# Logits with slots on partitions, slot sums in four column groups, and TensorE in the written order

## The chip, the cores and the metric

The kernel runs on one core of one Trainium2 chip. The metric is the device time in microseconds of one execution, inputs and output in the chip's memory. TensorE multiplies matrices (PE in the profile, its weight loads PEld), ScalarE (ACT), VectorE (DVE) and GpSimd (POOL) work on elements; here GpSimd issues all loads and SyncE (SP) the stores.

## The reference

Attention over a sliding window, and then a soft mixture of experts on its result:

```python
# q, k, v: 8 batches, 8 heads, 576 rows, 64 wide
scores = scale * q @ k.T, kept where 0 <= i - j < 64        # window
attn = softmax(scores) @ v
x = attn as (B*S, H*D) = (4608, 512)
logits = x @ phi                                            # phi: 512 x 32 (8 experts x 4 slots)
d = softmax of logits over the 4608 rows;  slot_input = d.T @ x      # 32 x 512
slot_out[e] = relu(slot_input[e] @ w1[e]) @ w2[e]           # w1: 512 x 1024, w2: 1024 x 512
c = softmax of logits over the 32 slots;   out = c @ slot_out        # 4608 x 512
```

## The kernel before

A **unit** is half a batch: four heads, 576 rows. There are 16, u = 2b + half. Each runs three **steps** j = 0, 1, 2 over windows of 64 queries (4, 4 and 1 windows). A step does `stage_t2` (transposes of v, line L177, copied to vw by L178), `stage_s` (a mask product, L188, and the scores, L195, summed in the one PSUM tile sc; then their exponential on ScalarE, L200, into pm), a third of the *next* unit's first transposes (`stage_t1`, L146: q in step 0, k in step 1, v in step 2; the copies out are L153 on ScalarE and for half of v L151 on VectorE), and `stage_av` of the step before (L223, then L229 to L241 on VectorE, into x_bp). So v of the next unit is transposed in step 2 and read by L177 at the next unit's start.

The mixture's work on a batch is cut into six pieces, one at the end of each step of the two units that follow: `stage_xt` three times (L258: transposes of x into xT), `stage_logit` (L269: 32 columns a matmul, rows on partitions; L273 exponential, written four times side by side into ex), `stage_slot` (L288: sums over the rows of ex times x and of ex times ones, 32 columns a matmul; L294 adds them to acc), `stage_et` (L301: ex transposed into ET). The last batch does them after the loop. An even batch has 4 chunks of 128 rows, an odd one 5. Then come the experts (L367, L374, L386 from the weights w1s and w2s; the last expert's w2 is w2l) and the output (L402 from ET, scaled by L406 and L408, stored by L411).

PSUM tiles tagged "tr" rotate over four buffers; sc and av have one each. A scheduler orders the instructions of each engine, but for those named in `manual_schedule`, which stay in the order in which the code issues them: GpSimd alone, before. Its queue holds the loads: `issue_loads(u)` issues q, k and v of unit u+3 and one half of an expert's weight, the rest of the weights all at unit 13.

Of the kernel before, what the change touches and what calls it, by code (L numbers as in the profile page):

```python
# [16 lines left out]
def kernel(  # L17
# [10 lines left out]
    nc = tc.nc  # L28

    B, H, S, Dh = q.shape  # L30
    D, NSLOT = moe_phi.shape
    E, _, F = moe_w1.shape
# [73 lines left out]
    ones = const.tile([128, 128], FP16, name="ones")  # L106
    nc.vector.memset(ones, 1.0)
# [19 lines left out]
    acc = const.tile([128, 5, NSLOT], FP32, name="acc")  # L127
# [118 lines left out]
    def moe_chunks(b):  # L246
        c = [4 * (b % 2) + i for i in range(4)]
        return c + [8] if b % 2 else c

    def stage_xt(b, part):  # L250
        xb = xbp[b // 2]
        ch = moe_chunks(b)[2 * part:2 * part + 2]
        if not ch:
            return
        tr = ps.tile([128, 8, 128], FP16, name="tr", tag="tr", bufs=4)
        for n, c in enumerate(ch):
            for kk in range(NHD):
                nc.tensor.transpose(tr[:, 4 * n + kk, :], xb[:, c, 128 * kk:128 * kk + 128], ident[:, :])  # L258
        xT = pxt.tile([128, 8, 128], FP16, name="xT", tag="xT")
        nc.vector.tensor_copy(out=xT[:, 0:4 * len(ch), :], in_=tr[:, 0:4 * len(ch), :])  # L260
        moe[b, part] = xT

    def stage_logit(b):
        ch = moe_chunks(b)
        lt = ps.tile([128, 5, NSLOT], FP32, name="lt", tag="tr", bufs=4)
        for n, c in enumerate(ch):
            xT = moe[b, n // 2]
            for kk in range(NHD):
                nc.tensor.matmul(lt[:, n, :], xT[:, 4 * (n % 2) + kk, :], phi_sb[:, kk, :],  # L269
                                 start=(kk == 0), stop=(kk == NHD - 1))  # L270
        nch = len(ch)
        ex = psm.tile([128, 5, 4, NSLOT], FP16, name="ex", tag="ex", bufs=2)
        nc.scalar.activation(ex[:, 0:nch, :, :],  # L273
                             lt[:, 0:nch, :].unsqueeze(2).broadcast_to([128, nch, 4, NSLOT]), AF.Exp)
        rs = psm.tile([128, 5], FP32, name="rs", tag="rs")
        nc.vector.reduce_sum(rs[:, 0:nch], ex[:, 0:nch, 0, :], axis=AXX)
        nc.vector.reciprocal(crcp[:, b, 0:nch], rs[:, 0:nch])
        moe["ex", b] = ex

    def stage_slot(b):  # L280
        ch = moe_chunks(b)
        xb = xbp[b // 2]
        ex = moe["ex", b]
        pa = ps.tile([128, 5, NSLOT], FP32, name="pa", tag="tr", bufs=4)
        for n, c in enumerate(ch):
            for dc in range(NHD + 1):
                lhs = xb[:, c, 128 * dc:128 * dc + 128] if dc < NHD else ones[:, :]
                nc.tensor.matmul(pa[:, dc, :], lhs, ex[:, n, 0, :],  # L288
                                 start=(n == 0 and dc == 0), stop=(n == len(ch) - 1 and dc == NHD),
                                 skip_group_check=True)  # L290
        if b == 0:
            nc.vector.tensor_copy(out=acc[:, :, :], in_=pa[:, :, :])
        else:
            nc.vector.tensor_tensor(out=acc[:, :, :], in0=pa[:, :, :], in1=acc[:, :, :], op=ALU.add)  # L294

    def stage_et(b):
        ex = moe["ex", b]
        nch = len(moe_chunks(b))
        te = ps.tile([128, 8, 128], FP16, name="te", tag="tr", bufs=4)
        for n in range(nch):  # L300
            nc.tensor.transpose(te[:, n, :], ex[:, n].rearrange("p r s -> p (r s)"), ident[:, :])  # L301
        nc.vector.tensor_copy(out=ET[:, 4 * b:4 * b + 4, :], in_=te[:, 0:4, :])
        if nch > 4:
            nc.vector.tensor_copy(out=ET[:, 4 * B + b // 2, :], in_=te[:, 4, :])


    nu = len(units)
# [13 lines left out]
    for u in range(nu):  # L321
        issue_loads(u)
        if u == nu - 3:
            while w_order:
                load_w(*w_order.pop(0))
        for j in range(3):
            stage_t2(u, j)
            stage_s(u, j)
            if u + 1 < nu:
                stage_t1(u + 1, j)  # L330
            if pend is not None:
                stage_av(*pend)
                pu, pj = pend
                if pj == 2 and units[pu][1] == 1:
                    b = units[pu][0]
                    todo += [lambda b=b: stage_xt(b, 0), lambda b=b: stage_xt(b, 1), lambda b=b: stage_xt(b, 2),
                             lambda b=b: stage_logit(b), lambda b=b: stage_slot(b), lambda b=b: stage_et(b)]
# [8 lines left out]
    stage_xt(b, 1)  # L346
    stage_xt(b, 2)
    stage_logit(b)
    stage_slot(b)
    stage_et(b)  # L350
# [4 lines left out]
    dinv = const.tile([128, NSLOT], FP32, name="dinv")  # L355
    nc.vector.reciprocal(dinv, acc[:, NHD, :])
    nc.vector.tensor_tensor(out=slot_inT[:, :, :], in0=acc[:, 0:NHD, :],
                            in1=dinv[:, :].unsqueeze(1).broadcast_to([128, NHD, NSLOT]), op=ALU.mult)
# [90 lines left out]
```

## Time and profile before

| | |
|---|---|
| three runs, median (lowest to highest) | 201.0 us (198.66 to 201.95) |
| the profiled execution: its time, its span | 200.05 us, 198.2 us |
| busy: TensorE, VectorE, ScalarE | 142.4, 109.3, 109.6 us |
| mean granted TensorE clock | 0.924 |
| loads on GpSimd's queue | 30.97 MB |
| TensorE matmuls (each with a weight load) | 3148 |

The span is from the first to the last instruction; the execution's own time has 1.85 us around it. Views of the trace are in us from the span's start. In the order of time a row has its start, its duration, engine, line, operation, output<-inputs, shapes and count, and in brackets how long the engine stood idle before it and for what. A matmul's duration holds some 0.18 us of latency, so matmuls in a row overlap and their spacing is what they cost. "issue" is time in which an engine waited for nothing that the profile shows.

### The profile page before, as it was taken

The numbers are of one execution on the slowest core, as the hardware profiler recorded it, in microseconds if no ns is written. First come the engines' busy times: TensorE is split into PE (matmuls) and PEld (weight loads), VectorE is DVE, ScalarE is ACT, GpSimd is POOL, SyncE is SP. The second block draws the span as 40 slices with busy tenths as digits, with TensorE's granted clock in tenths as the row PEclk, the third lists the DMA queues.
The fourth block names the chain that finished last, engine by engine and source line by source line (L and its number), as shares of the span: only waits on it lengthen the run. The fifth ranks groups of instructions, "written<-read, shape, count | busy, mean of one in ns | idle before, by whom it ended". The sixth has DMA issues, their size and how long they took to land.

```text
span 198.2 us, 7045 instructions
## 1 busy us (share of the span) xinstructions
PE 142.4 (72%) x3148; PEld 106.2 (54%) x3148; DVE 109.3 (55%) x268; ACT 109.6 (55%) x164; POOL 59.6 (30%) x89
## 2 busy tenths in 40 slices
PE   0599897778987879884999897698757873983000
PEld 0376776667766667764778676587644441220000
DVE  3026677558665757753787585578852112895000
ACT  2457976858575596765479486566311222894000
POOL 7945444423341424321442662222230000000000
PEclk9999999999999999998799999999985999698555
DMA  4999999999999999999699999999999992799995
GB/s 69 160 204 206 207 209 206 205 207 209 211 209 204 206 208 204 203 162 171 69 175 187 175 178 186 210 208 211 206 212 207 211 203 37 289 377 379 379 334 145
DMA packets 31309, 40.84 MB, mean 206 GB/s; under 512 B 2096, under 2 KB 22576, under 8 KB 31280
## 3 DMA queue, kind: packets, MB, share of 16 engines
q0 software_dynamic: 26384, 30.97, 93.5%
q1 hardware_dynamic: 4896, 9.44, 13.6%
q8 instruction: 24, 0.39, 0.7%
q14 instruction: 5, 0.04, 0.1%
HBM read 61.93 MB, written 9.44 MB: 360 GB/s over the span
## 4 chain that ended last, share of the span: by engine, by line
PE 43%; ACT 15%; DMA 13%; issue 11%; DVE 8%; POOL 1%; DVEq 0%; ACTq 0%; POOLq 0%
PE tr L146 11%; DMA w2l<-in_moe_w_dram 10%; PE tr L177 8%; ACT pm L200 7%; PE sc L188 6%; PE sc L195 5%; PE av L223 4%; DVE ob L408 4%; DMA kn<-in_k_dram 3%; ACT kT_125 L153 3%; PE tr L258 3%; ACT kT_116 L153 2%; PE cp L402 2%; PE lt L269 2%; ACT qT L153 2%
## 5 line engine op out<-in xcount | busy, mean ns | idle before, releaser
L200 ACT ACTIVATE pm<-sc 128x1024 f16<-128x1024 f32 (+1 forms) x48 | 39.5, 823 | 40.2 <-PE sc L195 37.4
L177 PE MATMUL tr<-ident,vT 128*128 128x128 f16 x288 | 24.9, 224 | 1.0 <-DVE rc L229 0.9
L153 ACT COPY qT<-tr 128x640 f16<-128x640 f16 (+1 forms) x32 | 21.9, 746 | 4.9 <-PE tr L146 4.9
L188 PE MATMUL sc<-rep,hide 64*128 64x512 f16 (+1 forms) x96 | 20.8, 339 | 2.5 <-ACT pm L200 1.3
L231 DVE TENSOR_TENSOR x_bp<-av,rc 128x512 f16<-128x512 f32 x32 | 22.0, 687 | 0.8
L177 PEld LDWEIGHTS <-vT 128*128 128x128 f16 x288 | 17.7, 100 | 4.8 <-issue 3.1
L223 PEld LDWEIGHTS <-pm 128*64 128x64 f16 x576 | 15.8, 112 | 6.9 <-issue 5.6
L151 DVE COPY vT<-tr 128x512 f16<-128x512 f16 x16 | 11.6, 724 | 12.9 <-PE tr L146 12.8
L61 POOL DMA_DIRECT2D vn<-in_v_dram x16 | 11.5, 716 | 23.0 <-PE av L223 14.6
L146 PE MATMUL tr<-ident,qn 128*64 128x128 f16 x288 | 12.3, 233 | 7.6 <-DMA qn<-in_q_dram 5.4
L61 POOL DMA_DIRECT2D qn<-in_q_dram x16 | 11.5, 717 | 20.7 <-PE av L223 14.2
L61 POOL DMA_DIRECT2D kn<-in_k_dram x16 | 11.5, 718 | 16.5 <-PE av L223 12.0
L178 DVE COPY vw_126<-tr 128x1024 f16<-128x1024 f16 (+1 forms) x24 | 13.3, 553 | 4.3 <-PE tr L177 4.2
L146 PE MATMUL tr<-ident,vn 128*64 128x128 f16 x288 | 13.8, 232 | 2.3 <-issue 0.7
L81 POOL DMA_DIRECT2D w1s<-in_moe_w_dram x16 | 11.5, 719 | 11.3 <-DMA w1s<-in_moe_w_dram 8.9
L178 DVE COPY vw_118<-tr 128x1024 f16<-128x1024 f16 (+1 forms) x24 | 13.2, 549 | 2.8 <-PE tr L177 2.8
L84 POOL DMA_DIRECT2D w2s<-in_moe_w_dram x14 | 10.6, 767 | 11.8 <-DMA w2s<-in_moe_w_dram 8.7
L146 PEld LDWEIGHTS <-qn 128*64 128x64 f16 x288 | 9.5, 117 | 8.5 <-DMA qn<-in_q_dram 5.4
L408 DVE TENSOR_SCALAR ob<-cp,crcp 128x512 f32<-128x512 f32 x18 | 12.6, 747 | 1.3 <-PE cp L402 1.0
L402 PE MATMUL cp<-slot_oa,ET 128*128 128x512 f16 x36 | 11.5, 425 | 2.4 <-ACT ob L406 1.3
L260 DVE COPY xT<-tr 128x1024 f16<-128x1024 f16 (+1 forms) x20 | 12.6, 628 | 1.0 <-PE tr L258 0.7
L146 PE MATMUL tr<-ident,kn 128*64 128x128 f16 x288 | 11.8, 228 | 1.8 <-DMA kn<-in_k_dram 1.8
(76 smaller groups left out, 258.2 us busy)
## 6 DMA issues: line engine op xcount, KB each, us to landing
out_dram<-ob SPq DMA_DIRECT2D x18, 512.0 KB, 5.5
w1s<-in_moe_w_dram POOLq DMA_DIRECT2D x16, 512.0 KB, 13.9
w2s<-in_moe_w_dram POOLq DMA_DIRECT2D x14, 512.0 KB, 13.5
qn<-in_q_dram POOLq DMA_DIRECT2D x16, 288.0 KB, 9.9
kn<-in_k_dram POOLq DMA_DIRECT2D x16, 288.0 KB, 9.6
vn<-in_v_dram POOLq DMA_DIRECT2D x16, 288.0 KB, 8.9
w2l<-in_moe_w_dram POOLq DMA_DIRECT2D x2, 512.0 KB, 19.7
phi_sb<-in_moe_phi_dram POOLq DMA_DIRECT2D x1, 32.0 KB, 7.8
```

The source lines that it names most:

```text
L61: nc.gpsimd.dma_start(out=t, in_=src[b, 4 * half:4 * half + 4].rearrange("(x h) (g t) d -> (h g) x (t d)", x=2, h=2, t=T))
L146: nc.tensor.transpose(tr[64 * x:64 * x + 64, j, :], src[:, x, 64 * (t0 + j):64 * (t0 + j) + 64], ident[:, :])
L153: nc.scalar.copy(out=o, in_=i)
L177: nc.tensor.transpose(tr[:, 2 * w + h, :], st["vT"][:, h, 64 * i:64 * i + 128], ident[:, :])
L178: nc.vector.tensor_copy(out=st["vw"][:, wins[0]:wins[0] + n, :, 0:64], in_=tr[:, 0:2 * n, :].rearrange("p (w h) (x d) -> p w (h x) d", h=2 ...
L188: nc.tensor.matmul(sc[:, x, 0:128 * n], hide[64 * x:64 * x + 64, :], rep[64 * x:64 * x + 64, 0:2 * n, :], start=True, stop=False, skip_gro ...
L200: nc.scalar.activation(pm[:, :, 0:2 * n, :], sc[:, :, 0:128 * n].rearrange("p x (w q) -> p x w q", q=64), AF.Exp, scale=scale)
L223: nc.tensor.matmul(av[r0:r0 + 64, kk, 65 * (w // 2):65 * (w // 2) + 65], pm[:, x, h * n + w, :], st["vw"][:, i, 2 * h + x, 0:65], start=Tr ...
L231: nc.vector.tensor_tensor(out=xb[:, c0:c0 + 2, 256 * half:256 * half + 256].rearrange("p c (k d) -> p k c d", d=64), in0=avv[:, :, :, 0:64 ...
L260: nc.vector.tensor_copy(out=xT[:, 0:4 * len(ch), :], in_=tr[:, 0:4 * len(ch), :])
L402: nc.tensor.matmul(cp[:, :], ET[:, 4 * blk + g, :], slot_oa[:, :], start=True, stop=True)
L408: nc.vector.tensor_scalar(out=ob[:, g, :], in0=cp[:, :], scalar1=cr, scalar2=None, op0=ALU.mult)
```

## The change

Seven things:

- **Logits** have slots on partitions: `stage_logit` multiplies phi4 (phi's 32 columns four times) with xT, 512 columns a matmul, four matmuls for a batch's first four chunks, and four of 128 columns for the fifth of an odd batch. The exponential goes straight into ET, and its sum over columns into esum. The layout of xT follows.
- **stage_ex** replaces stage_et, one piece earlier: matmuls of 32 columns turn ET's chunks back (te); ScalarE casts them to ex, VectorE sums them for crcp.
- **Slot sums** take ex (32 columns) as weights and x as the moving operand of 512 columns, chunk n in column group n % 4; acc is 128 x 512. The sums with ones are gone.
- **At the end** acc is scaled by 1/esum and the four groups are summed by four matmuls (si) with sel4 into slot_inT.
- **TensorE** joins GpSimd in `manual_schedule`.
- **Weights**: `issue_loads` issues two halves in place of one at u = 2, 5, 8 and 11.
- The pool of xT has one buffer of each tag in place of three.

```diff
-    pxt = ctx.enter_context(tc.tile_pool(name="pxt", bufs=3))
+    pxt = ctx.enter_context(tc.tile_pool(name="pxt", bufs=1))
...
+    sel4 = const.tile([128, NSLOT], FP16, name="sel4")
+        nc.vector.reduce_sum(sel4, ident.rearrange("p (g s) -> p s g", s=NSLOT), axis=AXX)
...
+    phi4 = const.tile([128, NHD, 4, NSLOT], FP16, name="phi4")
+    nc.vector.tensor_copy(out=phi4, in_=phi_sb.unsqueeze(2).broadcast_to([128, NHD, 4, NSLOT]))
...
-    psum1.enter_context(tc.manual_schedule(engines={mybir.EngineType.Pool}))
+    psum1.enter_context(tc.manual_schedule(engines={mybir.EngineType.Pool, mybir.EngineType.PE}))
...
     def stage_logit(b):
-        for n, c in enumerate(ch):
-            xT = moe[b, n // 2]
-            for kk in range(NHD):
-                nc.tensor.matmul(lt[:, n, :], xT[:, 4 * (n % 2) + kk, :], phi_sb[:, kk, :],
-                                 start=(kk == 0), stop=(kk == NHD - 1))
-        nc.scalar.activation(ex[:, 0:nch, :, :],
-                             lt[:, 0:nch, :].unsqueeze(2).broadcast_to([128, nch, 4, NSLOT]), AF.Exp)
+        for kk in range(NHD):
+            nc.tensor.matmul(lt[:, :], phi4[:, kk].rearrange("p r s -> p (r s)"), moe[b][:, kk],
+                             start=(kk == 0), stop=(kk == NHD - 1))
+        nc.scalar.activation(ET[:, 4 * b:4 * b + 4, :], lt[:, :].rearrange("p (c q) -> p c q", q=128),
+                             AF.Exp, accum_out=esum[:, b:b + 1])
+        if b % 2:
+            ...
+                nc.tensor.matmul(l8[:, :], phi4[:, kk].rearrange("p r s -> p (r s)"), moe[b, 8][:, kk],
+            ...
+            nc.scalar.activation(ET[:, 4 * B + b // 2, :], l8[:, :], AF.Exp,
+                                 accum_out=esum[:, B + b // 2:B + b // 2 + 1])
...
+    def stage_ex(b):
+        te = ps.tile([128, 5, NSLOT], FP32, name="te", tag="tr", bufs=4)
         for n, c in enumerate(ch):
+            nc.tensor.matmul(te[:, n, :], ET[:, c, :], ident[:, 0:NSLOT], start=True, stop=True)
+        nc.scalar.copy(out=ex[:, 0:nch, :], in_=te[:, 0:nch, :])
+        nc.vector.reduce_sum(rs[:, 0:nch], te[:, 0:nch, :], axis=AXX)
         nc.vector.reciprocal(crcp[:, b, 0:nch], rs[:, 0:nch])
...
     def stage_slot(b):
         for n, c in enumerate(ch):
-            for dc in range(NHD + 1):
-                lhs = xb[:, c, 128 * dc:128 * dc + 128] if dc < NHD else ones[:, :]
-                nc.tensor.matmul(pa[:, dc, :], lhs, ex[:, n, 0, :], ...
+            g = n % 4
+            nc.tensor.matmul(pa[32 * g:32 * g + 32, :], ex[:, n, :], xbp[b // 2][:, c, :],
+                             start=(n < 4), stop=(n + 4 >= len(ch)), skip_group_check=True)
...
-    def stage_et(b):
...
-            load_w(*w_order.pop(0))
+            for _ in range(2 if u % 3 == 2 else 1):
+                load_w(*w_order.pop(0))
...
+    nc.vector.reduce_sum(dinv[:, 0:1], esum[:, :], axis=AXX)
+    nc.vector.reciprocal(dinv[:, 1:2], dinv[:, 0:1])
+    nc.scalar.activation(pa_sb[:, 0:256], acc[:, 0:256], AF.Copy, scale=dinv[:, 1:2])
+    nc.vector.tensor_scalar(out=pa_sb[:, 256:512], in0=acc[:, 256:512], scalar1=dinv[:, 1:2], scalar2=None, op0=ALU.mult)
...
+    for dc in range(NHD):
+        nc.tensor.matmul(si[:, dc, :], pa_sb[:, 128 * dc:128 * dc + 128], sel4[:, :], start=True, stop=True)
+    nc.vector.tensor_copy(out=slot_inT, in_=si)
```

TensorE has 6298 instructions before and 5826 after. How they stand changes at three places of which the prediction speaks. Lines of attention are 5 higher in the changed kernel (L177 is L182, L188 L193, L195 L200, L200 L205, L223 L228).

TensorE at the boundary from unit 2 to unit 3, before: hide and rep make the mask product, kT and qT the scores, vT the transposes that read both copies of v. "..." stands for more of the same row.

```order
L223 MATMUL av<-vw_118,pm 64x65
L188 LDWEIGHTS hide
L188 MATMUL sc<-rep,hide 128x512
...
L195 LDWEIGHTS kT_125
L195 MATMUL sc<-qT,kT_125 128x64
...
L177 LDWEIGHTS vT
L177 MATMUL tr<-ident,vT 128x128
```

The same place in the change:

```order
L228 MATMUL av<-vw_118,pm 64x65
L182 LDWEIGHTS vT
L182 MATMUL tr<-ident,vT 128x128
...
L193 LDWEIGHTS hide
L193 MATMUL sc<-rep,hide 128x512
...
L200 LDWEIGHTS kT_125
L200 MATMUL sc<-qT,kT_125 128x64
```

Two mask products and three score products have moved from ahead of the eight transposes of vT to behind them. At boundaries into even units, before, one mask product stood ahead of the transposes and one behind.

ScalarE in an odd unit (u = 5, batch 1), before, from one first pm to the next:

```order
L200 ACTIVATE pm<-sc 128x1024
L153 COPY qT<-tr 128x128x5
L153 COPY qT<-tr 128x128x4
L273 ACTIVATE ex<-lt 128x640
L200 ACTIVATE pm<-sc 128x1024
L153 COPY kT_116<-tr 128x2x64x5
L153 COPY kT_116<-tr 128x2x64x4
L200 ACTIVATE pm<-sc 128x2x128
L153 COPY vT<-tr 128x2x64x5
```

and in the change:

```order
L205 ACTIVATE pm<-sc 128x1024
L158 COPY qT<-tr 128x128x5
L158 COPY qT<-tr 128x128x4
L280 ACTIVATE ET,esum<-lt 128x512
L287 ACTIVATE ET,esum<-l_1356 128x128
L205 ACTIVATE pm<-sc 128x1024
L158 COPY kT_116<-tr 128x2x64x5
L158 COPY kT_116<-tr 128x2x64x4
L301 CAST ex<-te 128x160
L205 ACTIVATE pm<-sc 128x2x128
L158 COPY vT<-tr 128x2x64x5
```

One exponential has become two, and a cast stands ahead of the third pm.

VectorE at the end, from the last batch's first xT copy to the experts' input, before:

```order
L260 COPY xT<-tr 128x1024
L237 RECIPROCAL rc<-av 64x4
L260 COPY xT<-tr 128x1024
L238 TENSOR_TENSOR x_bp<-av,rc 64x256
L260 COPY xT<-tr 128x512
L276 TENSOR_REDUCE rs<-ex 128x5
L277 RECIPROCAL crcp<-rs 128x5
L294 TENSOR_TENSOR acc<-pa,acc 128x160
L302 COPY ET<-te 128x512
L304 COPY ET<-te 128x128
L356 RECIPROCAL dinv<-acc 128x32
L357 TENSOR_TENSOR slot_inT<-acc,dinv 128x128
```

and in the change:

```order
L319 TENSOR_TENSOR acc<-pa,acc 128x512
L242 RECIPROCAL rc<-av 64x4
L268 COPY xT<-tr 128x4x256
L243 TENSOR_TENSOR x_bp<-av,rc 64x256
L268 COPY xT<-tr 128x4x256
L272 COPY xT_3698<-tr 128x512
...
L303 TENSOR_REDUCE rs<-te 128x5
L304 RECIPROCAL crcp<-rs 128x5
L319 TENSOR_TENSOR acc<-pa,acc 128x512
L373 TENSOR_SCALAR slot_oa<-acc,dinv 128x256
L381 CAST slot_inT<-si 128x128
```

The first acc of the change is that of batch 6, now ahead of the last batch's xT copies; the copies to ET are gone, and the scaling and the copy of si have come.

More of the change, by code (lines that the diff above doesn't have):

```diff
@@ L105 @@
             in_=ident[64 * h:64 * h + 64, 64 * h:64 * h + 64].unsqueeze(1).broadcast_to([64, 8, 64]))
-    ones = const.tile([128, 128], FP16, name="ones")
-    nc.vector.memset(ones, 1.0)
+    sel4 = const.tile([128, NSLOT], FP16, name="sel4")
+    with nc.allow_low_precision("sums of 0 and 1"):
+        nc.vector.reduce_sum(sel4, ident.rearrange("p (g s) -> p s g", s=NSLOT), axis=AXX)
     kTs, vTs, vws, hTs = [], [], [], []
@@ L254, in stage_xt @@
             return
+        nch = len(ch)
+        if part == 0:
+            moe[b] = pxt.tile([128, NHD, 4, 128], FP16, name="xT", tag="xT")
         tr = ps.tile([128, 8, 128], FP16, name="tr", tag="tr", bufs=4)
-        for n, c in enumerate(ch):
-            for kk in range(NHD):
-                nc.tensor.transpose(tr[:, 4 * n + kk, :], xb[:, c, 128 * kk:128 * kk + 128], ident[:, :])
-        xT = pxt.tile([128, 8, 128], FP16, name="xT", tag="xT")
-        nc.vector.tensor_copy(out=xT[:, 0:4 * len(ch), :], in_=tr[:, 0:4 * len(ch), :])
@@ new lines, in stage_xt, with stage_logit @@
+        if part < 2:
+            nc.vector.tensor_copy(out=moe[b][:, :, 2 * part:2 * part + 2, :],
+                                  in_=tr[:, :, :].rearrange("p (k n) q -> p k n q", n=2))
+        else:
+            moe[b, 8] = pxt.tile([128, NHD, 128], FP16, name="xT8", tag="xT8")
+            nc.vector.tensor_copy(out=moe[b, 8], in_=tr[:, 0:4, :])
+    def stage_logit(b):
+        lt = ps.tile([128, 512], FP32, name="lt", tag="tr", bufs=4)
+        for kk in range(NHD):
+            nc.tensor.matmul(lt[:, :], phi4[:, kk].rearrange("p r s -> p (r s)"), moe[b][:, kk],
[3 more added lines that the diff above has]
+        if b % 2:
+            l8 = ps.tile([128, 128], FP32, name="l8", tag="tr", bufs=4)
+            for kk in range(NHD):
+                nc.tensor.matmul(l8[:, :], phi4[:, kk].rearrange("p r s -> p (r s)"), moe[b, 8][:, kk],
+                                 start=(kk == 0), stop=(kk == NHD - 1))
+            nc.scalar.activation(ET[:, 4 * B + b // 2, :], l8[:, :], AF.Exp,
+                                 accum_out=esum[:, B + b // 2:B + b // 2 + 1])
@@ L280, in stage_slot @@
     def stage_slot(b):
+        ex = moe["ex", b]
+        pa = ps.tile([128, D], FP32, name="pa", tag="tr", bufs=4)
         ch = moe_chunks(b)
-        xb = xbp[b // 2]
-        ex = moe["ex", b]
-        pa = ps.tile([128, 5, NSLOT], FP32, name="pa", tag="tr", bufs=4)
         for n, c in enumerate(ch):
-            for dc in range(NHD + 1):
-                lhs = xb[:, c, 128 * dc:128 * dc + 128] if dc < NHD else ones[:, :]
-                nc.tensor.matmul(pa[:, dc, :], lhs, ex[:, n, 0, :],
-                                 start=(n == 0 and dc == 0), stop=(n == len(ch) - 1 and dc == NHD),
-                                 skip_group_check=True)
+            g = n % 4
+            nc.tensor.matmul(pa[32 * g:32 * g + 32, :], ex[:, n, :], xbp[b // 2][:, c, :],
+                             start=(n < 4), stop=(n + 4 >= len(ch)), skip_group_check=True)
         if b == 0:
-            nc.vector.tensor_copy(out=acc[:, :, :], in_=pa[:, :, :])
+            nc.vector.tensor_copy(out=acc[:, :], in_=pa[:, :])
         else:
-            nc.vector.tensor_tensor(out=acc[:, :, :], in0=pa[:, :, :], in1=acc[:, :, :], op=ALU.add)
-    def stage_et(b):
[L297 to L304, printed above, removed]
+            nc.vector.tensor_tensor(out=acc[:, :], in0=pa[:, :], in1=acc[:, :], op=ALU.add)
     nu = len(units)
```

29 lines of the change are left out of this document (14 added, 15 removed).

## The prediction

> **What bounds the kernel now.** I read the slices first, then the sums over stretches, the waits, ScalarE's order of time, and last the chain. Of the page, the data rate in 40 slices, the queue that carries instructions, and the chain's shares:
>
> ```profile
> GB/s 69 160 204 206 207 209 206 205 207 209 211 209 204 206 208 204 203 162 171 69 175 187 175 178 186 210 208 211 206 212 207 211 203 37 289 377 379 379 334 145
> q8 instruction: 24, 0.39, 0.7%
> PE 43%; ACT 15%; DMA 13%; issue 11%; DVE 8%; POOL 1%; DVEq 0%; ACTq 0%; POOLq 0%
> ```
>
> Loads run flat at about 207 GB/s, except from slice 17 to 24. The stretches (last three columns: clock, DMA share, GB/s):
>
> ```profile
> 30.00:81.00 51.00, 42.23 (x1093) 34.25 (x1086) 33.95 (x80) 35.08 (x52) 17.90 (x25) 1.00 1.20 207
> 81.00:104.00 23.00, 18.77 (x448) 15.26 (x446) 14.83 (x36) 14.06 (x22) 7.84 (x11) 0.93 1.00 153
> 49.67:54.70 5.03, 5.03 (x128) 3.97 (x127) 3.17 (x8) 2.70 (x4) 1.78 (x3) 1.00 1.18 211
> ```
>
> No engine is full: in 51 us TensorE has 42.2 busy, ScalarE 35.1. So I look at who waits. The largest wait, then ScalarE in order of time over an even and an odd unit:
>
> ```profile
> ACT pm L200 <- PE sc L195: 37.4, 27, 3.5
> ```
>
> ```profile
> 97.28 1.02 ACT L200 ACTIVATE pm<-sc 128x1024 f16<-128x1024 f32 x1 [2.85 <-PE sc L195]
> ...
> 104.25 1.02 ACT L200 ACTIVATE pm<-sc 128x1024 f16<-128x1024 f32 x1 [1.48 <-PE sc L195]
> 105.17 1.37 ACT L153 COPY qT<-tr 128x640 f16<-128x640 f16 x2
> 106.37 0.63 ACT L273 ACTIVATE ex<-lt 128x512 f16<-128x512 f32 x1
> 106.85 1.07 ACT L200 ACTIVATE pm<-sc 128x1024 f16<-128x1024 f32 x1
> ...
> 112.71 1.02 ACT L200 ACTIVATE pm<-sc 128x1024 f16<-128x1024 f32 x1 [2.64 <-PE sc L195]
> ```
>
> The even unit (97.28 to 104.25) takes 6.97 us: ScalarE works through without a gap and then waits once, 1.48 us, for the next unit's scores. The odd unit takes 8.46, with the exponential of the logits (L273) more. So the period is **ScalarE's work plus one bubble at the unit's end**, plus what stalls TensorE. Those stalls, in the chain: its first and last piece named "issue" between 30 and 143 us, and the longest of 15, together 15.4 us:
>
> ```profile
> 30.97 0.70 issue
> 89.88 2.61 issue
> 139.55 0.75 issue
> ```
>
> Between two of them lie 256 instructions: the stretch 49.67:54.70 runs from one to the next with 128 matmuls and 127 weight loads. The instruction queue's 0.39 MB in 24 pieces are 16 KB each, so I read a piece as 256 instructions and the stall as the wait for it.
>
> The weights end last, but hardly. The last expert's two halves:
>
> ```profile
> 163.37 0.40 PE L386 MATMUL sop<-w2l,hT_140 128*32 128x512 f16 x4 [0.15 <-DMA w2l<-in_moe_w_dram]
> 165.91 0.40 PE L386 MATMUL sop<-w2l,hT_140 128*32 128x512 f16 x4 [2.14 <-DMA w2l<-in_moe_w_dram]
> ```
>
> Without the load the second group would follow at about 163.8: only 2.1 to 2.5 us hang on DMA.
>
> **The change part by part.** Terms are against the profiled execution, 200.05 us (span 198.2).
>
> *Weights two at a time.* Four weight loads move from the tail to units 2, 5, 8 and 11. The stretch 81:104 moved 153 GB/s, where 207 was to be had: 23 x 54/207 = 6.0 us lost there, more up to slice 24. Four loads of 512 KB are 10 us of queue, so the last weights land 6 to 9 us sooner, before 160, and the wait of 2.5 goes: **-2.5**. Late next is TensorE's own path, and if the terms below hold (+3.7 on it) even weights at 165.9 would not be waited for. SyncE's queue is not touched. Do q, k and v come late behind them on GpSimd's queue?
>
> ```profile
> qn<-in_q_dram POOLq DMA_DIRECT2D x16, 288.0 KB, 9.9
> ```
>
> They are issued when unit u-3's buffer is free, so about three periods of 7 us ahead, and land after 9.9: some 11 us of slack against at most 10 us of added queue, spread over the program. I cost it at nothing; were that cover gone, an odd 2 us at one unit.
>
> *MoE on TensorE.* Prices, from the order of time:
>
> ```profile
> 86.63 0.67 PE L269 MATMUL lt<-phi_sb,xT 128*128 128x32 f16 x20
> 87.15 0.61 PE L177 MATMUL tr<-ident,vT 128*128 128x128 f16 x8
> 87.69 0.39 PE L188 MATMUL sc<-rep,hide 64*128 64x512 f16 x2
> 87.91 0.40 PE L195 MATMUL sc<-qT,kT_125 64*128 64x64 f16 x16
> ```
>
> Twenty logit matmuls hold TensorE 0.52 us (86.63 to 87.15); 512 columns hold it 0.22 (87.69 to 87.91, two in different halves of the rows). New logits: 4 x 0.22 = 0.88, plus 4 of 128 columns (0.22) in odd batches; old 0.42 and 0.52: about +0.5. Against it, from the chain:
>
> ```profile
> 89.19 0.70 PE pa L288 x24
> 128.48 0.39 PE te L301 x5
> 165.91 0.42 PE sop L386 x4
> ```
>
> Slot sums were 0.5 to 0.7; four in column groups are, by the sop row, 0.42 with the latency, and if the groups did not overlap 4 x 0.22 = 0.88. The transposes te shrink from 128 columns to 32, -0.2. TensorE's sum per batch lies between -0.1 and +0.6; ScalarE's row of work hides it, except behind a stall. I take 0 here, and keep +2 over seven batches for the upper end.
>
> *MoE on ScalarE*, where nothing hides it. By form:
>
> ```profile
> L273 ACT ACTIVATE ex<-lt 128x640 f16<-128x640 f32 x4 | 2.9, 720 | 4.9 <-PE lt L269 4.9
> L273 ACT ACTIVATE ex<-lt 128x512 f16<-128x512 f32 x4 | 2.5, 624 | 0.0
> L371 ACT ACTIVATE h_sb<-hp 128x256 f16<-128x256 f32 x8 | 3.1, 383 | 12.4 <-PE hp L367 12.4
> L294 DVE TENSOR_TENSOR acc<-pa,acc 128x160 f32<-128x160 f32 x7 | 2.2, 318 | 3.9 <-PE pa L288 3.9
> L231 DVE TENSOR_TENSOR x_bp<-av,rc 128x512 f16<-128x512 f32 x32 | 22.0, 687 | 0.8
> ```
>
> Each batch adds a cast of 128 or 160 columns, each odd one an exponential of 128. No row has 128 columns: above is 0.38 (256), below, from 720 - 624 = 96 ns for 128 columns more, 0.1. Back to back an instruction costs less than its row (512 columns: 106.37 to 106.85, 0.48). I take 0.22. Seven batches lie in the loop: 7 x 0.22 + 3 x 0.22, less 3 x 0.1 (640 to 512) = 1.9; where a stall already left ScalarE idle it is free, so **+1.3**, between 0 and 10 x 0.38 = 3.8. The accumulated sum of the exponential is in no row: nothing, or at most another 0.1 on each; a gain is excluded since the work is added. VectorE gains (no copies of ET) and loses (acc 318 to 687 ns); it is not late.
>
> *The order of attention.* The boundary between units, before:
>
> ```profile
> 135.46 0.76 ACT L153 COPY vT<-tr 128x640 f16<-128x640 f16 x1
> 135.69 0.73 DVE L151 COPY vT<-tr 128x512 f16<-128x512 f16 x1
> 136.53 0.46 PEld L177 LDWEIGHTS <-vT 128*128 128x128 f16 x8 [0.38 <-ACT vT L153]
> 137.57 1.02 ACT L200 ACTIVATE pm<-sc 128x1024 f16<-128x1024 f32 x1 [1.35 <-PE sc L195]
> ```
>
> L177 waits for both copies, of which VectorE's ends last (136.42). Before, the two mask matmuls (L188) and at times three of L195 filled that wait; now they stand behind L177, and pm waits for them: 0.22 + 0.06 later at most, so 0.2 at each of the 7 boundaries into units 3 to 15, +1.4. At the others one mask matmul stood ahead of L177 and one behind; now both stand behind, and as they use different halves of the rows the pair takes the 0.22 that one took: 0. At the start the same as at the 7, at a low clock:
>
> ```profile
> 12.07 1.01 PE L177 MATMUL tr<-ident,vT 128*128 128x128 f16 x8
> 13.28 1.02 ACT L200 ACTIVATE pm<-sc 128x1024 f16<-128x1024 f32 x1 [1.76 <-PE sc L195]
> ```
>
> Fifteen score matmuls, done by 12.07 before, now follow L177: +0.6. **+2.0** together, between 0 and 3; it cannot gain, since the same work stands later.
>
> *Fewer instructions.* 6298 to 5826 is 1.8 pieces of 256, at 15.4/15 = 1.0 us a stall: -1.8; but the two pieces due in the quiet DMA stretch (near 95 and 102) showed none, and with DMA full there I expect one of them: **-0.8**, between -3 and +1.5.
> The Trainium skill ("Runtime: NRT & Kernel Launch", Instruction fetch mechanics) says that instructions come in blocks of 16 KiB, 256 of them, and that crossing a block is mostly hidden. The rows agree with the spacing and not with the hiding; by the page this term is 0, and the sum 0.8 higher.
>
> *The tail.* The last batch has nothing beside it:
>
> ```profile
> 145.68 0.42 DVE L260 COPY xT<-tr 128x512 f16<-128x512 f16 x1 [0.38 <-PE tr L258]
> 149.78 1.68 PE L367 MATMUL hp<-w1s,slot_inT 128*32 128x256 f16 x25 [1.23 <-DVE slot_inT L357]
> ```
>
> From the end of that copy (146.10) to the experts are 3.7 us. Now the accumulation of batch 6 (0.69) stands ahead of the xT copies on VectorE, logits take 0.88 + 0.2, exponential 0.62 + 0.22, te 0.3, cast 0.3, slot sums 0.6, acc 0.69, scaling 0.4, the matmuls si 0.3, the copy to slot_inT 0.2. Logits need only the second xT copy, at about 145.9: 145.9 + 4.8 = 150.7, so +0.9; short bursts at a low clock may add half a microsecond: **+1.2**, between 0.5 and 2.
>
> Sum: -2.5 + 1.3 + 2.0 - 0.8 + 1.2 = **+1.2**, 201.25 in the terms of that execution. The median of the runs, 201.0 (198.66 to 201.95), lies 0.95 above it, which would give 202.2; the lowest run lies 1.4 below it. I keep near that execution and forecast 201.3: no change.
>
> **The rivals.**
> *ScalarE takes all of it (slower).* Place: odd units. Price: casts and exponentials at the 256-column row, 3.8, with 0.1 more for each accumulated sum (1.0), and +2 of TensorE behind stalls. It decides if ScalarE has no idle time ahead of the third pm of an odd unit. 201.25 - 1.3 + 6.8 = 206.75. For: every unit without a stall shows ScalarE without a gap. Against: 15.4 us of stalls leave holes.
>
> *The stalls shrink (faster).* If fewer instructions, and another position against ScalarE's work, cut the 15.4 to 10: 201.25 + 0.8 - 5.4 = 196.65; to 9, 195.65. The 2.61 alone, with the low clock behind it (0.93 from 81 to 104), is some 3 of them. Against: DMA is now full throughout, and the stalls were seen where it is full.
>
> *The loads do not do what they are moved for.* Four double loads push q, k or v past their use, 1 us at each: 205.25. Against: the 11 us of slack.
>
> **How the numbers follow.** Forecast 0.64 (198.5 to 204.0); ScalarE 0.17; stalls 0.15; loads 0.04. A measurement tells about 2% here, 4 us. Faster, under 197.0: the stalls' case and a little of the forecast's edge, 0.17. Slower, over 205.0: ScalarE's case, half of the loads', less where only part of it comes, 0.18. The range, 196.0 to 205.5, takes in the milder stalls' case and ScalarE's up to 5 of its 6.8, and leaves out about 2 in 10.
>
> **What would show it.** Loads flat near 207 GB/s until about 157 us, no wait of sop for w2l; the bubble before the first pm of odd units 1.5 to 1.7 us; casts near 0.28 us; issue stalls every 256 instructions, about as long as now; from the last xT copy to the first expert near 5 us. It is wrong if the stalls go or double, or if q, k or v are waited for.

## The result, and the profile after

| | before | after |
|---|---|---|
| median on the same chip (lowest to highest, 4 runs each) | 201.42 us (198.66 to 201.95) | 192.42 us (191.73 to 192.63) |
| the profiled execution: its time, its span | 200.05, 198.2 us | 191.73, 189.9 us |
| first pm of the last unit (u = 15) | 137.57 | 129.57 |
| from there to the first hp of the experts | 12.2 us | 14.8 us |
| from there to the end of the last sop | 16.5 us | 13.7 us |
| from there to the end of the span | 31.9 us | 31.8 us |

The change is faster: ratio 0.9623, 95% interval 0.9518 to 0.9729. The ratios, here and in the table of the experiments, leave out runs more than 1.5% above the fastest of their kernel, here two of before (201.84 and 201.95). The forecast of 201.3 us and its range down to 196.0 were wrong. Below, pm is the exponential of attention's scores, hp the experts' first product, hT its result turned round, and sop the product of hT with the second weights. In the profiled executions attention gives 8.0 us (the third row), the stretch to the experts costs 2.6, and the experts up to the last sop take 2.8 less. Together that is 8.2, the difference of the two spans within 0.1.

The page of the changed kernel, the lines that answer to those of before: the data rate in 40 slices, the queue that carries instructions, the chain's shares by engine and by line:

```profile
GB/s 62 169 202 206 207 209 206 206 212 208 207 207 206 213 205 207 207 206 212 205 207 206 207 209 208 207 212 208 209 208 209 209 144 3 372 376 381 380 337 145
q8 instruction: 23, 0.38, 0.7%
PE 34%; ACT 21%; DVE 14%; DMA 14%; issue 7%; POOL 1%; DVEq 0%; ACTq 0%; POOLq 0%
```

The loads are flat, as forecast. What was not forecast is "issue": from 11% of the chain to 7%. The chain itself, its pieces named "issue" after the first 30 us (start, length):

```profile
30.82 0.75 issue
60.85 1.69 issue
79.87 0.63 issue
86.01 0.55 issue
109.70 0.70 issue
121.85 0.71 issue
136.29 1.48 issue
```

The last of these stands between GpSimd's issue of w2l and that load, and is not TensorE's. The other six make 5.0 us together; the chain of before had 15 of them, 15.4 us. Where the time went is best seen by the **rhythm** of the stalls. In the order of time of TensorE's weight loads, before, four of the rows that stood idle for "issue" (the last column, in brackets):

```profile
31.67 0.15 PEld L195 LDWEIGHTS <-kT_116 64*128 64x128 f16 x4 [0.83 <-issue]
...
37.73 0.09 PEld L195 LDWEIGHTS <-kT_125 64*128 64x128 f16 x1 [1.19 <-issue]
...
43.75 0.53 PEld L146 LDWEIGHTS <-qn 128*64 128x64 f16 x17 [0.87 <-issue]
...
49.67 0.26 PEld L223 LDWEIGHTS <-pm 128*64 128x64 f16 x11 [0.74 <-issue]
```

They end 6.06, 6.02 and 5.92 us apart, whether the stall took 0.74 or 1.19. And in the change, the stretches between two stalls (columns: stretch, its length, busy time of PE with its matmuls in brackets, of PEld with its weight loads, of DVE, ACT and POOL, then clock, DMA share, GB/s):

```profile
31.56:43.23 11.67, 10.16 (x255) 8.01 (x255) 8.12 (x21) 8.31 (x15) 4.86 (x7) 1.00 1.21 208
43.51:55.20 11.69, 10.74 (x255) 8.52 (x256) 7.67 (x17) 9.25 (x18) 4.80 (x7) 1.00 1.19 208
62.54:79.87 17.33, 15.24 (x383) 12.29 (x383) 12.73 (x30) 12.30 (x22) 6.47 (x9) 1.00 1.19 208
86.56:109.70 23.14, 21.25 (x511) 16.46 (x510) 17.80 (x41) 17.65 (x30) 9.44 (x14) 1.00 1.20 207
```

Two pieces of 256 in 11.7 us, three in 17.3, four in 23.1: 5.8 us each, without the stall that ends each stretch. With it, the stalls' ends from 31.56 to 122.55 are 15 pieces in 90.99 us, 6.07 each. The places are set by the count: in both kernels the first stall at 31 us stands behind some 955 of TensorE's records, and every later one that is listed here some multiple of 255 to 256 on, whatever stands there. So the kernel gets 256 TensorE instructions every 6.0 us, before and after. Where attention needs them faster, that is its period, and the stall is only what is left of 6.0 us after the work.

The same stretch, from the first pm of unit 3 to that of unit 15, in both kernels:

```profile
34.50:137.57 103.07, 85.64 (x2182) 69.81 (x2178) 68.03 (x163) 69.60 (x102) 36.79 (x51) 0.98 1.14 190
```

```profile
34.59:129.57 94.98, 82.45 (x2002) 64.75 (x1998) 66.93 (x154) 70.62 (x121) 36.73 (x51) 1.00 1.20 208
```

4360 instructions in 103.07 us are 6.05 us for 256; 4000 in 94.98 are 6.08. 360 fewer at 6.05 make 8.5 us; 8.1 came. ScalarE does 1.0 us more work in 8.1 us less.

### The profile page after: what moved, and what is told of

It reads as the page before. It is cut to its first block, busy times and chain, and to the rows that moved or that the text cites. A ratio compares the mean times of both kernels' runs of the same rounds, so it can differ in the third digit from the quotient of the medians.

```text
span 189.9 us, 6582 instructions
## 1 busy us (share of the span) xinstructions
PE 137.8 (73%) x2912; PEld 99.3 (52%) x2912; DVE 108.5 (57%) x259; ACT 111.7 (59%) x189; POOL 59.6 (31%) x89
## 4 chain that ended last, share of the span: by engine, by line
PE 34%; ACT 21%; DVE 14%; DMA 14%; issue 7%; POOL 1%; DVEq 0%; ACTq 0%; POOLq 0%
DMA w2l<-in_moe_w_dram 10%; ACT pm L205 9%; PE tr L182 8%; PE tr L151 8%; DVE ob L431 6%; PE sc L193 5%; DVE vT L156 4%; PE sc L200 4%; ACT kT_125 L158 3%; DMA vn<-in_v_dram 3%; ACT kT_116 L158 3%; ACT qT L158 3%; PE tr L266 3%; PE av L228 3%; PE lt L278 2%
## 5 line engine op out<-in xcount | busy, mean ns | idle before, releaser
L205 ACT ACTIVATE pm<-sc 128x1024 f16<-128x1024 f32 (+1 forms) x48 | 39.4, 821 | 32.6 <-PE sc L200 32.6
L182 PE MATMUL tr<-ident,vT 128*128 128x128 f16 x288 | 24.8, 223 | 7.5 <-DVE rc L234 4.8
L182 PEld LDWEIGHTS <-vT 128*128 128x128 f16 x288 | 18.2, 99 | 12.7 <-ACT vT L158 11.3
L228 PEld LDWEIGHTS <-pm 128*64 128x64 f16 x576 | 15.6, 111 | 6.1 <-issue 4.6
L193 PE MATMUL sc<-rep,hide 64*128 64x512 f16 (+1 forms) x96 | 16.6, 337 | 1.6 <-ACT pm L205 0.9
L151 PE MATMUL tr<-ident,vn 128*64 128x128 f16 x288 | 12.8, 227 | 3.2 <-ACT kT_116 L158 1.6
L234 DVE RECIPROCAL rc<-av 128x8 f32<-128x8 f32 x32 | 6.3, 196 | 13.6 <-PE av L228 13.5
L158 ACT COPY vT<-tr 128x640 f16<-128x640 f16 x16 | 12.7, 791 | 0.3 <-PE tr L151 0.3
L151 PEld LDWEIGHTS <-vn 128*64 128x64 f16 x288 | 10.2, 113 | 4.7 <-issue 3.0
## 6 DMA issues: line engine op xcount, KB each, us to landing
w1s<-in_moe_w_dram POOLq DMA_DIRECT2D x16, 512.0 KB, 15.5
```

The source lines that it names most:

```text
L151: nc.tensor.transpose(tr[64 * x:64 * x + 64, j, :], src[:, x, 64 * (t0 + j):64 * (t0 + j) + 64], ident[:, :])
L158: nc.scalar.copy(out=o, in_=i)
L182: nc.tensor.transpose(tr[:, 2 * w + h, :], st["vT"][:, h, 64 * i:64 * i + 128], ident[:, :])
L193: nc.tensor.matmul(sc[:, x, 0:128 * n], hide[64 * x:64 * x + 64, :], rep[64 * x:64 * x + 64, 0:2 * n, :], start=True, stop=False, skip_gro ...
L205: nc.scalar.activation(pm[:, :, 0:2 * n, :], sc[:, :, 0:128 * n].rearrange("p x (w q) -> p x w q", q=64), AF.Exp, scale=scale)
L228: nc.tensor.matmul(av[r0:r0 + 64, kk, 65 * (w // 2):65 * (w // 2) + 65], pm[:, x, h * n + w, :], st["vw"][:, i, 2 * h + x, 0:65], start=Tr ...
```

## The experiments

Three theories: **pace** (each 256 TensorE instructions cost 6.0 us while the loads are full; the mixture's smaller count is the gain), **order** (the order of TensorE as written), **loads** (the weights issued earlier). The comparison with the kernel before is made on the same chip; there it took 198.9 us (e1 to e4), 198.93 (e5 to e9) and 199.46 (e10 to e12). The last three columns are from the row of the same stretch, first pm of unit 3 to first pm of unit 15, in each kernel's profile.

| | us, median (lowest to highest) | ratio to before [95%] | stretch, us | TensorE instructions in it | us for 256 |
|---|---|---|---|---|---|
| before | | | 103.07 | 4360 | 6.05 |
| the change | 192.42 (191.73 to 192.63) | 0.9623 [0.9518, 0.9729] | 94.98 | 4000 | 6.08 |
| e1 order alone | 200.85 (200.16 to 202.12) | 1.0142 [1.0052, 1.0231] | 104.79 | 4360 | 6.15 |
| e2 weights alone | 197.78 (196.68 to 199.2) | 0.9989 [0.9937, 1.0041] | 106.91 | 4360 | 6.28 |
| e3 change, free order | 191.65 (191.29 to 192.58) | 0.9664 [0.96, 0.9728] | 94.94 | 4000 | 6.08 |
| e4 mixture alone | 192.42 (192.19 to 192.8) | 0.9698 [0.9644, 0.9751] | 94.92 | 4000 | 6.07 |
| e5 before, fewer instructions | 193.01 (192.21 to 193.41) | 0.9708 [0.9639, 0.9778] | 94.61 | 3988 | 6.07 |
| e7 change, more instructions | 201.17 (200.7 to 201.33) | 1.0127 [1.0046, 1.0208] | 101.63 | 4324 | 6.02 |
| e8 change, more TensorE time | 192.6 (191.62 to 193.97) | 0.9698 [0.961, 0.9785] | 95.35 | 4000 | 6.10 |
| e9 change, weights late | 219.84 (one run) | | 90.20 | 4002 | 5.77 |
| e10 change, no mask product | 191.94 (191.41 to 192.06) | 0.9723 [0.9618, 0.9828] | 92.54 | 3856 | 6.14 |
| e11 change, two loads fewer | 192.49 (189.97 to 193.51) | 0.9714 [0.949, 0.9938] | 95.33 | 4000 | 6.10 |
| e12 both | 189.94 (188.75 to 191.66) | 0.9571 [0.9322, 0.9821] | 94.20 | 3856 | 6.25 |

### Which part does it: e1 to e4

e1 is the kernel before with TensorE's order as written:

```diff
-    psum1.enter_context(tc.manual_schedule(engines={mybir.EngineType.Pool}))
+    psum1.enter_context(tc.manual_schedule(engines={mybir.EngineType.Pool, mybir.EngineType.PE}))
```

> The kernel before with TensorE in the written order and nothing else (6298 TensorE instructions, as before). Theory pace: from 30 us to the end of attention TensorE gets a piece of 256 instructions every 6.0 us and no faster, so the number of its instructions sets the time. Then this stays at 199 to 202 us, the first pm of the last unit at 136 to 139 us. Theory order: the written order is what gains; then 193 to 195 us. Theory loads: the earlier weights are what gains; then 200 to 202 us.

e2 is the kernel before with the weights two at a time:

```diff
-            load_w(*w_order.pop(0))
+            for _ in range(2 if u % 3 == 2 else 1):
+                load_w(*w_order.pop(0))
```

> The kernel before with two weight halves at every third unit and nothing else. Pace: attention as long as before, first pm of the last unit at 136 to 139 us, and only the wait for the last weights goes: 198 to 200 us. Loads: 193 to 195 us, the first pm of the last unit near 130 us. Order: 199 to 201 us.

e3 is the change with TensorE's order left to the scheduler; e4 is e3 with one weight at a time as well, so the new mixture alone:

```diff
-    psum1.enter_context(tc.manual_schedule(engines={mybir.EngineType.Pool, mybir.EngineType.PE}))
+    psum1.enter_context(tc.manual_schedule(engines={mybir.EngineType.Pool}))
```

```diff
-            for _ in range(2 if u % 3 == 2 else 1):
-                load_w(*w_order.pop(0))
+            load_w(*w_order.pop(0))
```

> The change with TensorE left to the scheduler again (5826 TensorE instructions). Pace: 191 to 193.5 us, as the change. Order: 199 to 201 us. Loads: 192 to 193 us.

> The change with TensorE left to the scheduler and one weight half a unit: only the mixture's new form and its 472 fewer TensorE instructions are left. Pace: the first pm of the last unit at 129 to 132 us, as in the change; the loads run dry in between, so that the last weights are waited for, 193 to 198 us in all. Order and loads: the first pm of the last unit at 136 to 139 us, 199 to 201 us.

The mixture alone gives the whole gain, as far as the measurement tells: 192.42 us in e4, its stretch 94.92. The order alone costs 1.4% (0.5 to 2.3), with a granted clock of 0.93 in its stretch where before had 0.98, so how much of that is the order isn't shown; taking it out of the change (e3) gives nothing that the measurement tells (191.65 against 192.42). The weights alone give nothing: in e2 the last of them landed at 157.69 in place of 165.86, but attention ran no faster, so nothing waited for them any more and nothing came sooner. Some expectations of pace missed narrowly: the first pm of the last unit came at 140.47 in e1 and 140.57 in e2 (136 to 139 expected), e2's time lies just under 198, and e4's just under 193. That stretch of e2:

```profile
33.66:140.57 106.91, 91.14 (x2182) 73.94 (x2178) 68.77 (x163) 69.25 (x102) 40.08 (x56) 0.92 1.19 208
```

208 GB/s in place of 190, the same count, and 3.8 us longer than before; but the granted clock was 0.92 in place of 0.98, so what of it is due to the loads isn't shown. The theories order and loads fall as the cause.

### Count or time of TensorE: e5, e7, e8

e5 leaves work out of the kernel before: three of four logit matmuls of a chunk, and the slot sums of all chunks but the first. The rest of the old mixture, its exponential and its copies stay.

```diff
-            for kk in range(NHD):
+            for kk in range(1):
                 nc.tensor.matmul(lt[:, n, :], xT[:, 4 * (n % 2) + kk, :], phi_sb[:, kk, :],
-                                 start=(kk == 0), stop=(kk == NHD - 1))
+                                 start=True, stop=True)
...
+        ch = ch[0:1]
         for n, c in enumerate(ch):
```

> The kernel before with 496 TensorE instructions left out: the logits take one of four parts of the contraction, the slot sums the first chunk alone. Order, loads and all work of the other engines are as before. Pace: 1.9 pieces fewer, the first pm of the last unit 7 to 11 us earlier (127 to 131 us), and 192 to 197 us in all, by how late the last weights are. Order and loads: what is left out lay beside ScalarE's work, so 198 to 201 us.

e7 does each matmul of te seven times, e8 makes each of them 384 columns wide (idw is the identity's 32 columns and zeros):

```diff
-            nc.tensor.matmul(te[:, n, :], ET[:, c, :], ident[:, 0:NSLOT], start=True, stop=True)
+            for _ in range(7):
+                nc.tensor.matmul(te[:, n, :], ET[:, c, :], ident[:, 0:NSLOT], start=True, stop=True)
```

```diff
-            nc.tensor.matmul(te[:, n, :], ET[:, c, :], ident[:, 0:NSLOT], start=True, stop=True)
+            nc.tensor.matmul(te[:, NSLOT * n:NSLOT * n + 384], ET[:, c, :], idw[:, :], start=True, stop=True,
+                             skip_group_check=True)
```

> The change with each of the small matmuls te done seven times: 432 more TensorE instructions, 216 matmuls at some 25 ns each, 5.4 us of TensorE. Pace: 1.7 pieces more at 6.0 us, 200 to 203 us. A rival, that it is TensorE's time that counts: at most 5.4 us more, 192.5 to 197 us.

> The change with each te matmul 384 columns wide in place of 32, the rest of them unused: 36 matmuls at some 0.14 us more, 4.9 us of TensorE, and not one instruction more. Pace: 192 to 193.5 us, no change. The rival, that it is TensorE's time that counts: as the run with more instructions, 195 to 197 us.

The same stretch of e5, of e7 and of e8:

```profile
34.32:128.93 94.61, 81.00 (x1996) 64.86 (x1992) 68.13 (x163) 68.84 (x103) 36.52 (x51) 1.00 1.19 206
```

```profile
34.90:136.53 101.63, 86.91 (x2164) 69.27 (x2160) 68.31 (x154) 71.58 (x121) 38.95 (x54) 0.98 1.20 208
```

```profile
34.86:130.21 95.35, 86.79 (x2002) 67.23 (x1998) 67.84 (x154) 70.94 (x121) 36.82 (x52) 0.98 1.20 208
```

e5 and the change reach the same time with the same count and quite different mixtures. e7 and e8 give TensorE the same busy time, 86.9 and 86.8 us; only e7 has more instructions, and only e7 is slow, 101.63 us against 95.35. The **count** decides, not the time. 324 instructions more at 6.08 would be 7.7 us; 6.7 came.

### Does the pace hang on the loads: e9

e9 issues the weights, but for one half in unit 0 and the one ahead of the loop, after the last q, k and v, so that attention's loads run alone:

```diff
-            for _ in range(2 if u % 3 == 2 else 1):
+            if u == 0:
```

> The change with all weights but the first two halves loaded after the last q, k and v, so that attention runs with light loads (about 130 GB/s in place of 207). The total is long, 215 to 225 us, as the weights come late; what counts is attention. If a piece of instructions takes 6.0 us because its transfer stands behind the loads, the stalls go and the first pm of the last unit comes at 120 to 126 us. If 6.0 us is its own pace, the stalls stay 6.0 us apart and it comes at 128 to 131 us.

Its time of 219.84 us, from a single run, holds the weights at the end; what counts is attention. The data rate, the stretch, and the longest pieces named "issue" of its chain up to 121 us:

```profile
GB/s 79 166 203 206 209 206 207 147 121 137 115 115 126 134 121 114 117 122 122 147 189 208 210 210 210 206 210 208 212 205 210 208 208 148 99 376 378 380 356 146
```

```profile
36.78:126.98 90.20, 81.13 (x2002) 64.96 (x2000) 66.38 (x153) 70.47 (x120) 29.50 (x41) 0.99 0.97 143
```

```profile
31.93 1.02 issue
...
56.60 0.12 issue
...
86.38 0.12 issue
```

While the loads are full there is a stall, the last at 31.93. At 114 to 147 GB/s none is over 0.12 us, over eleven pieces. The stretch shrinks to 90.2 us for the same instructions: the work that stays when instructions come in time. The first pm of the last unit came at 126.98, between the two ranges that were expected: unit 3 began 2.2 us later than in the change, and the loads were full again from some 112 us on.

The traces also record each packet of the instruction queue (q8 on the page), which the views above don't list; each carries 16,384 bytes. Before, over the nine pieces that begin between 31 and 80 us, the next packet starts 3.55 to 3.74 us after a piece has begun, takes 0.89 to 0.97 us, and the first instruction behind it comes 1.32 to 1.61 us after its end: 3.6 + 0.9 + 1.4 make up the 6.0 us. With light loads in e9 the packet itself is no shorter (0.89 to 1.35 us), but from 40 to 104 us it starts at most 3.1 us after a piece has begun, at times as soon as it begins, and lands 1.5 to 4.4 us before its instructions run. So I read the 6.0 us as the time that the next 256 instructions need to reach TensorE while the loads fill the DMA engines, 3.6 us of it spent before their packet starts; the 5.77 us for 256 here are those of the work itself. What the packet waits for isn't shown. When the loads are full again the packets stand 5.9 to 6.0 us apart once more, but no stall at a piece's start shows up to the end of attention; why not isn't shown.

### What bounds the kernel next: e10 to e12

e10 leaves the mask product out (scores are not masked), e11 the loads of the last expert's second weights (the expert takes those of the one before), e12 both:

```diff
-        for x in range(2):
-            nc.tensor.matmul(sc[:, x, 0:128 * n], hide[64 * x:64 * x + 64, :],
-                             rep[64 * x:64 * x + 64, 0:2 * n, :], start=True, stop=False,
-                             skip_group_check=True)
```

```diff
-    w_order = [(e, n) for e in range(E) for n in range(4)]
+    w_order = [(e, n) for e in range(E) for n in range(4)][:-2]
...
+    w2_t[E - 1] = w2_t[E - 2]
```

> The change with the mask products left out (L193; scores are not masked): 192 TensorE instructions fewer, 0.75 of a piece of 256, and nothing else changed. Pace theory: at 6.0 us a piece the first pm of the last unit comes 3 to 4.5 us earlier than 129.57, at 125 to 126.5. Had a piece only the price of its stall, 1.0 us, it would come at 128.5 to 129. What sets the end is told apart too: if the last weights do (flat at 207 GB/s they land near 157.6 whatever attention does), the time stays at 191 to 192.5; if attention's end does, it falls with it, to 188 to 189.5.

> The change with both halves of the last expert's second weights not loaded (it uses those of the expert before it): 1 MB less, 5 us of queue at 207 GB/s, TensorE's work and its instructions as in the change. If the loads set the end by the 1.1 to 1.2 us for which sop waits, and no more: the first pm of the last unit stays at 129.6, the last load lands near 152.5, sop waits no more, 190.8 to 191.6. If what follows attention sets the end alone: 192.4, no change.

> Both edits: mask products left out and the last expert's second weights not loaded. If attention is paced by instructions and the end is set by whichever comes last, attention's chain or the last weights: the first pm of the last unit at 125 to 126.5, and now the end follows, 187 to 188.5, 3 to 4.5 under the kernel without the loads alone. If something else holds the end (the tail's own work on another resource): 190.5 or more.

The first pm of the last unit came at 126.66 in e10, 2.9 us sooner: more than the 0.6 to 1.1 that the price of a stall would give, and just short of the 3 to 4.5 at 6.0 us a piece. (The mask products' own time on TensorE, 4.9 us less in the stretch, left with them, so e10 alone doesn't tell count from time; e7 and e8 do.) The time stayed at 191.94. The end of e10 in the order of time:

```profile
155.12 0.40 PE L405 MATMUL sop<-w2l,hT 128*32 128x512 f16 x4 [1.05 <-DMA w2l<-in_moe_w_dram]
157.66 0.40 PE L405 MATMUL sop<-w2l,hT 128*32 128x512 f16 x4 [2.15 <-DMA w2l<-in_moe_w_dram]
```

Now the last weights set the end: the last sop ends at 158.06, as in the change. Without them and with the mask (e11) the median gains nothing either: 192.49 (189.97 to 193.51). In its profile the last sop ends at 158.95 without a wait, because the experts' own chain comes as late; the first pm of the last unit had come at 130.78, 1.2 us later than in the change. I had expected 1.1 us from the wait in the change; its row shows that it is shorter:

```profile
156.96 0.19 DVE L402 CAST hT_143<-th 128x32 f16<-128x32 f32 x1 [1.07 <-PE th L397]
157.20 0.86 PE L409 MATMUL sop<-w2l,hT_143 128*32 128x512 f16 x8
```

The last hT is ready at 157.15 and the second half of w2l at 157.62: of the 0.86 us perhaps 0.2 are a wait. Only with both gone does the median move, to 189.94; its runs spread from 188.75 to 191.66 and overlap those of e11, so this is the least sure of the results. The forecast of 187 to 188.5 for e12 missed by 1.4 us: attention won 2.1 us against the change in place of 3 to 4.5, and 0.7 of it went again in a tail of 15.5 us. Its stretch is only 0.8 us shorter than the change's, 6.25 us a piece. The packets of the instruction queue show where that went: three in this stretch started 4.8 to 5.0 us after the piece before had begun in place of 3.6, two in e10's and one in the change's. Why some come later isn't shown. So the profile of the change shows **two chains that end within a microsecond of each other**, and the runs suggest that neither a shorter attention nor earlier weights alone would make it faster. No run pointed to a version that beats the change and computes the same.

## Why the prediction was wrong, point by point

- **Fewer instructions: the step that failed.** The prediction found the pieces of 256 and that TensorE waits for them, and then priced a piece at its stall: "6298 to 5826 is 1.8 pieces of 256, at 15.4/15 = 1.0 us a stall", and took -0.8, between -3 and +1.5. The price is the period, 6.0 us: in the measured stretch 360 instructions, 1.4 pieces, gave 8.1 us. A stall is what is left of the period after the work; work added or removed beside it changes the stall, a removed instruction changes the number of periods. The trace of before had shown it (in the rows of TensorE's weight loads above): the stalls ended 6.0 us apart although they differed in length, and the stretch of 5.03 us between two of them was quoted without adding the stall behind it. (The two pieces without a stall begin at 99.27 and 104.50, not near 95 and 102.) For the same reason the period was not "ScalarE's work plus one bubble at the unit's end": the wait of 2.64 us at the end of the odd unit that it showed follows a stall of TensorE for instructions, 0.69 us up to 110.30. By the rule of the Trainium skill that the prediction set beside this term ("Runtime: NRT & Kernel Launch", Instruction fetch mechanics: crossing a block of instructions is mostly hidden), the term would be 0; the trace of before already spoke against that, and e7 shows 6.7 us for 324 instructions.
- **The rival "the stalls shrink"** had the right direction and place, and a chance of 0.15. Its price, 5.4 us, was a guess at stall lengths, and too small; it did not see that the shorter count fixes the gain. What it took to speak against itself, that DMA is full throughout, held, but the pieces of the change still came 6.08 us apart, against 6.05 before.
- **MoE on ScalarE.** The casts took 0.26 to 0.31 us, as forecast (0.28). An accumulated sum has a row of its own that no row of before showed, 0.19 to 0.24 us, twice the bound:

```profile
139.75 0.60 ACT L280 ACTIVATE ET<-lt 128x512 f16<-128x512 f32 x1 [6.12 <-PE lt L278]
140.24 0.19 ACT L280 ACTIVATION_READ_ACCUMULATOR ET<-lt 128x1 f32 x1
```

  ScalarE's 1.0 us more in the stretch (69.60 to 70.62) is not seen in the time: behind the pace it has 24 us of idle time there. The rival "ScalarE takes all of it" fell with that.
- **The order of attention.** The bubble before the first pm of an odd unit, from unit 3 on, is 1.60 to 2.07 us, at or above the 1.5 to 1.7 that were forecast; into even units it is 1.43 to 1.67. One of each:

```profile
97.86 1.02 ACT L205 ACTIVATE pm<-sc 128x1024 f16<-128x1024 f32 x1 [1.74 <-PE sc L200]
...
105.80 1.02 ACT L205 ACTIVATE pm<-sc 128x1024 f16<-128x1024 f32 x1 [1.47 <-PE sc L200]
```

  The +2.0 is near what e1 shows where the order is alone (200.85 against 198.9, a ratio of 1.4%), though at a lower clock. In the change it is hidden in attention: with and without it the stretch is 94.98 and 94.94 us. The sum added terms that lie beside a period that none of them sets.
- **Weights two at a time.** The number of -2.5 came out (the first hp to the last sop takes 2.8 us less, the last half landed at 157.62, forecast about 157), and TensorE did not wait for q, k and v more than before. But that it is these weight loads that bring it is luck. Before, the last half landed at 165.86; two at a time with the old mixture (e2) brought it to 157.69, the new mixture with one at a time (e4) to 158.32, and both (e3) to 157.60. So beside the faster attention the two at a time are worth 0.7 us. The last sop waits for the load in e4 and in e3, here in this order:

```profile
158.36 0.40 PE L408 MATMUL sop<-w2l,hT 128*32 128x512 f16 x4 [1.71 <-DMA w2l<-in_moe_w_dram]
```

```profile
157.64 0.40 PE L409 MATMUL sop<-w2l,hT 128*32 128x512 f16 x4 [1.49 <-DMA w2l<-in_moe_w_dram]
```

  In the change, whose last half lands as in e3, the wait is short because the first hp comes 1.5 us later (144.37 against 142.82). Alone (e2) two at a time gave nothing in time.
- **The tail** was mis-sized: +1.2 forecast, +2.6 measured from the first pm of the last unit to the first hp. The order of operations is as worked out; their prices were taken at full clock, and the rows of the stretch show half:

```profile
137.80:144.40 6.60, 4.10 (x26) 1.53 (x29) 2.51 (x8) 1.75 (x6) 0.73 (x1) 0.50 1.19 208
```

```profile
137.85 1.86 PE L278 MATMUL lt<-xT,phi_133 128*128 128x512 f16 x4 [0.43 <-DVE xT L268]
...
141.34 1.03 PE L314 MATMUL pa<-x_bp,ex 128*32 128x512 f16 x5 [0.38 <-ACT ex L301]
...
144.37 0.62 PE L390 MATMUL hp<-w1s,slot_inT 128*32 128x256 f16 x8 [0.38 <-DVE slot_inT L381]
```

  A granted clock of 0.50 (0.71 in the answering stretch of before, 146.1 to 149.8): the four logit matmuls of 512 columns take 1.86 us with their latency and not 0.88 and some 0.2, the slot sums take 1.03 and not 0.6, and 4.8 us from logits to hp became 6.5. Since the loads end at 157.62 in any case, little of it is in the time: e10, whose tail starts 2.9 us sooner, is no faster.

With the price of 6.05 us on the instructions counted in attention (-8.5), nothing for what lies beside the pace, -2.5 for the weights and +2.6 for the tail, the prediction's own sum would have been -8.4, 191.6 in the terms of the profiled execution, which took 191.73. That is worked out with hindsight, from the measured sizes, and so close a match is partly luck. The last weights land 8.2 us sooner (157.62 against 165.86) and allow no more.

## What to carry to other kernels

Where an engine stalls at regular distances, measure the distance, not only the stall: if the distances are equal while the stalls differ, something is supplied at that rate, and each unit of it that is no longer needed is worth a whole distance. Terms of engines that wait within such a period add nothing to the time, so the sum has to be made from what sets the period, and the others only tell where it stops (here 90.2 us of 95.0). Then look at the end for a second chain: here the last weights and the experts end within a microsecond, and shortening one alone gave nothing that the runs tell.

## What was not expected of the hardware

- 256 TensorE instructions, matmuls and weight loads together, took 6.0 to 6.3 us on average over attention in twelve kernels with loads at 190 to 208 GB/s, and came without a visible wait at 114 to 147 GB/s (e9). The packet that brings them takes 0.9 of the 6.0 us; 3.6 pass before it starts.
- An accumulated sum on ScalarE takes a row of its own of 0.19 to 0.24 us behind its activation.
- TensorE's granted clock fell to 0.50 in the 6.6 us of the tail in which it was busy 62% of the time (4.10 of 6.60), having had 1.00 in attention.
